# A fused attention and mixture-of-experts kernel: another order of its first loads and of its last block's tail tiles

## The chip, the cores and the metric

The kernel runs on one core of one Trainium2 chip. Its time is the device time of one execution in microseconds (us), as the median of several runs; lower is better. Five engines work side by side, each with its own queue of instructions: TensorE (PE; its weight loads are shown as PEld), VectorE (DVE), ScalarE (ACT), GpSimd (POOL) and SyncE (SP), which here issues nearly all DMA transfers. They wait for each other by semaphores. One execution was also recorded by the hardware profiler, and all rows below come from that one.

## What is computed

Three steps follow each other. Attention over 4 batches of 8 heads, 576 tokens and a head width of 64, where each query keeps only its 32 largest scores; a gated product; and a mixture of 8 experts of which each token takes one:

```python
scores = q @ k.T / sqrt(D)
kth    = partition(scores, -32)[..., -32]
attn   = softmax(where(scores >= kth, scores, -1e9))
x      = (attn @ v), heads side by side          # 2304 x 512
x      = ((x @ w_a) * (x @ w_b)) @ w_out         # inner width 1536
logits = normalized(x) @ normalized(expert_emb).T / tau
e      = argmax(logits); gate = softmax(logits)[e]
out    = gate * (relu(x @ w1[e]) @ w2[e])        # inner width 1024
```

## The kernel before

**The attention loop.** `SEQ` names eight parts, in order: block (batch) 0 to 3, with A for the first 256 queries, B for the second 256, and T for the 64 tail queries. Each part runs over four pairs of heads. One query tile of 128 scores rows against 576 keys is called an attention tile here (the code says row); there are 144, taken one per step from step −10 on. A tail tile holds both heads of a pair, 64 queries each. Each step does several things for several tiles at once: `prep` (loads of keys and queries, ten steps ahead), `split_qk` (POOL splits keys and queries into a high and a low half; for the very first part ScalarE and VectorE do it, L255, L256), `turn_qk` (TensorE transposes them, L307), `scores` (TensorE L364, ScalarE's copy L365), `topk` (VectorE's chain of four MAX8, L385, and three MATCH_REPLACE8, L388), `softmax` (ScalarE L397, POOL L400, ScalarE L402), `turn` (TensorE transposes the weights of the softmax, L419, ScalarE copies them, L422), `mix` (TensorE multiplies with v, L460, and spreads the sums, L440) and `finish` (POOL scales and splits; the halves are written to memory as `xh_d` and `xl_d`, L482 and L483). A part with tail has 320 columns in `mix`, one without has 256. `finish` of a part's fourth pair raises `ready`, the count of tokens that are complete.

**The weights.** `Blocks` loads 36 tiles of 512 KB of 64-bit weights (L512), unpacks them on VectorE, ScalarE and POOL (L532 to L539), splits them with two matmuls (L550, L551) and stores them in `wab_d`.

**The gated product.** The 2304 tokens are cut into nine groups of 256 (groups 0 to 8). `moe1` multiplies a group: for each of 12 values of f it does 24 matmuls (L683) with the weights that are loaded again from `wab_d` (L620, four buffers `wab`), and two f later six matmuls of the second product (L652, three for each of two token tiles). `background` puts these matmuls between those of the attention, as far as a budget for the step allows. A group enters its list as soon as `ready` covers it, and may begin two steps later. Its inputs are then read from `xh_d` and `xl_d` (L608), into tiles called `raw64` for odd groups and `xg` for even ones; the first matmul of a group needs the low halves. What is left after the attention runs behind it, densely.

**The router.** `route` is a generator with one stage per `yield`; `background` advances it by one stage after some amount of TensorE work. It takes a finished tile of 128 tokens: transposes (L725), logits (L730), ScalarE's copy `lg` (L733), VectorE's reciprocal, maximum and index (L735 to L740), one-hot (POOL), ranks by matmuls (L754, L755), and a scatter of token numbers into the experts' lists (POOL L770). When all 18 tiles are through, the lists are read back and the tokens of each expert are gathered (POOL L1042), while the first expert's matmuls (L1080, L1092, L1186) begin.

**What sets the order.** TensorE, VectorE, ScalarE and POOL run in the order in which the program is written. SyncE doesn't: a scheduler places the DMA issues by readiness and by a priority, which `tc.high_priority(offset=...)` raises. An issue whose tile isn't free yet holds all that stand behind it on that queue.

Of the kernel before, what the change touches and what calls it, by code (L numbers as in the profile page):

```python
# [16 lines left out]
AF = mybir.ActivationFunctionType  # L17
# [7 lines left out]
CAP = 336  # L25
GROUPS = [(256 * i, 256) for i in range(9)]
GN = 256
SEQ = "0A 0BT 1A 1BT 2A 2BT 3AT 3B"
LAG = 2
AHEAD_L = 10  # L30
TL = 4
# [43 lines left out]
FG = 100000  # L75
# [7 lines left out]
def fused_kernel(  # L83
# [18 lines left out]
    pe, dve, act, pool, sp = nc.tensor, nc.vector, nc.scalar, nc.gpsimd, nc.sync  # L102
# [43 lines left out]

    order_of_parts = [(int(x[0]), x[1:]) for x in SEQ.split()]
    blocks = {"A": range(4), "B": range(4, 8), "T": (8,)}
# [14 lines left out]
    eps = cst.tile([P, 1], F32, name="eps")  # L163
# [5 lines left out]

    enT = cst.tile([P, KC, EW], F32, name="enT")  # L170
    dve.memset(enT, 0.0)

    def en_load(mk):
        e_sb = mk.tile([P, RW], F32, name="xr")[:NE, :DM]
        sp.dma_start(e_sb, emb)
        sp.dma_start(tau1, tau.unsqueeze(0).to_broadcast([P, 1]))
        e_sq = mk.tile([P, RW], F32, name="xr")[:NE, :DM]
        e_ss = cst.tile([NE, 2], F32, name="e_ss")
        act.activation(e_sq, e_sb, AF.Square, accum_out=e_ss[:, 0:1])
        pool.tensor_tensor(e_ss[:, 1:2], e_ss[:, 0:1], half[:NE], op=OP.pow)  # L180
        return e_sb, e_ss
# [16 lines left out]
    with ExitStack() as ph:  # L198
# [72 lines left out]
        def prep(b, pr, part, n, c0):  # L271
            o = Part()
            o.b, o.pr, o.n, o.c0 = b, pr, n, c0
            o.first = now[0] + AHEAD_L
            o.lead = part == [p for bb, p in order_of_parts if bb == b][0]
            o.tail = "T" in part
            o.M = 256 if "A" in part or "B" in part else 0
            o.N = o.M + 64 * o.tail
            o.c = 2 if "B" in part else 0
            if o.lead:  # L280
                load_k(o, b, pr)
            o.qr = load_q(o)
            o.qs = None
            return o
# [426 lines left out]
        def route(ch, p):  # L711
# [20 lines left out]
            lg = mk.tile([P, NE], F32, name="lg")  # L732
            act.activation(lg, pl[:, :NE], AF.Copy)  # L733
            yield 0.0
            dve.reciprocal(st[:, 1:2], st[:, 1:2])  # L735
            m8 = mk.tile([P, 8], F32, name="m8")
            dve.max(m8, lg)
# [49 lines left out]
        made = {}  # L787
# [76 lines left out]
        for step in range(-AHEAD_L, NRW + TL + 5):  # L864
            now[0] = step
            if step + AHEAD_L < NRW:
                b, pr, part, first, last, kind, c, slot = rows[step + AHEAD_L]
                if first:
                    with tc.high_priority(offset=FG):
                        o = made[b, pr, part] = prep(b, pr, part, len(made), c0)  # L870
                        coming.append(o)
                    if pr == NP - 1:
                        c0 += o.N
# [435 lines left out]
```

## Time and profile before

| | us |
|---|---|
| median of 3 runs (1329.62 to 1331.72) | 1330.2 |
| the profiled execution | 1327.13 |
| its span, first to last instruction | 1325.2 |
| TensorE busy | 1181.8 (89%) |
| VectorE busy | 920.5 (69%) |
| ScalarE busy | 820.3 (62%) |
| POOL busy | 715.1 (54%) |

A share is a mean over the whole span; the attention takes up the first 900 us, the rest of the gated product runs to about 1040 us and the experts from there on, and each has limits of its own. The mean granted clock of TensorE was 0.956 of full speed.

### The profile page before, as it was taken

Reading aid. Unit: us, or ns where it says so; the run is one execution under the profiler, and the core shown is the slowest. Engines: PE = TensorE matmul, PEld = TensorE weight load, DVE = VectorE, ACT = ScalarE, POOL = GpSimd, SP = SyncE. Lnnn points to the kernel's source line nnn. Section 1 sums busy time; section 2 is a strip of 40 time slices with the busy share of each in tenths; the row PEclk is TensorE's granted clock in tenths of the full one; section 3 lists DMA queues with packets and bytes.
Section 4 is the critical chain, followed back from the end, with each engine's and each line's share of the span. In section 5 each row is a group of like instructions: output and inputs, shape, how many; then the busy total and the mean of one; then the engine's idle time right before and its main releaser. Section 6 shows DMA issues by size and latency. Waiting matters only on the chain. (4 is left out here: it accounts for less than half of the span.)

```text
span 1325.2 us, 23082 instructions
## 1 busy us (share of the span) xinstructions
PE 1181.8 (89%) x7828; PEld 992.9 (75%) x7829; DVE 920.5 (69%) x1991; ACT 820.3 (62%) x1953; POOL 715.1 (54%) x1160
## 2 busy tenths in 40 slices
PE   4767878987999998999999998799999989999996
PEld 3444756666888787887887787678898868888885
DVE  6989999987899988998889899750100135444440
ACT  4776888876777777776778776663532335444441
POOL 4555767755676777765767766564455321111100
PEclk9786999897999999998999999799999999999999
DMA  6333476454666666665666656457998145555520
GB/s 210 121 103 124 143 244 210 177 179 146 182 184 223 185 208 193 212 180 176 204 183 192 202 165 203 146 170 247 331 300 246 40 129 197 174 168 173 176 91 19
DMA packets 125707, 237.00 MB, mean 179 GB/s; under 512 B 22765, under 2 KB 71021, under 8 KB 125586
## 3 DMA queue, kind: packets, MB, share of 16 engines
q1 hardware_dynamic: 121426, 225.20, 53.8%
q0 software_dynamic: 4160, 10.29, 2.4%
q8 instruction: 63, 1.03, 0.3%
q14 instruction: 58, 0.48, 0.1%
HBM read 195.38 MB, written 40.85 MB: 178 GB/s over the span
## 5 line engine op out<-in xcount | busy, mean ns | idle before, releaser
L385 DVE MAX8 t<-y 128x8 f32<-128x576 f32 x432 | 312.0, 750 | 3.1
L400 POOL TENSOR_TENSOR z<-s,z 128x576 f32<-128x576 f32 x144 | 206.2, 1432 | 105.6 <-ACT z L397 103.4
L683 PE MATMUL ab<-xg,wab 128*128 128x256 f32 x1440 | 215.8, 292 | 5.6 <-ACT gab L687 3.8
L388 DVE MATCH_REPLACE8 y<-t,y 128x576 f32<-128x576 f32 x288 | 214.0, 743 | 0.0
L683 PEld LDWEIGHTS ab<-xg,wab 128*128 128x128 f32 x1440 | 190.5, 193 | 9.0 <-ACT gab L687 4.4
L683 PE MATMUL ab<-raw,wab 128*128 128x256 f32 x1152 | 173.6, 292 | 6.8 <-ACT gab L687 4.4
L419 PE MATMUL tr<-ident,z 128*128 128x128 f32 x720 | 136.0, 289 | 44.5 <-ACT z L402 36.1
L402 ACT ACTIVATE z<-z,bi 128x576 f32<-128x576 f32 x144 | 111.6, 775 | 79.5 <-POOL z L400 79.4
L683 PEld LDWEIGHTS ab<-raw,wab 128*128 128x128 f32 x1152 | 152.4, 193 | 10.8 <-ACT gab L687 5.7
L385 DVE MAX8 t<-s 128x8 f32<-128x576 f32 x144 | 107.7, 748 | 54.1 <-ACT s L365 48.8
L364 PE MATMUL tr<-kT,qT 128*128 128x288 f32 x512 | 127.8, 334 | 18.1 <-ACT s L365 13.9
L422 ACT ACTIVATE wt<-tr 128x384 f32<-128x384 f32 (+2 forms) x320 | 127.4, 413 | 17.7 <-PE tr L419 16.9
L365 ACT ACTIVATE s<-tr 128x288 f32<-128x288 f32 x288 | 118.9, 413 | 30.0 <-PE tr L364 28.6
L419 PEld LDWEIGHTS tr<-ident,z 128*128 128x128 f32 x720 | 91.6, 147 | 60.2 <-ACT z L402 39.7
L652 PE MATMUL x<-wo,gh 128*128 128x512 f32 x432 | 135.6, 395 | 0.0
L1015 DVE TENSOR_TENSOR u<-raw,u 128x1024 fp32r<-128x1024 f32 x64 | 76.2, 1221 | 83.5 <-ACT u L1014 60.6
L1064 POOL DMA_INDIRECT out_dram<-o,ids x24 | 24.0, 1000 | 200.4 <-ACT o L1063 197.1
L1092 PE MATMUL y<-u,hT 128*128 128x512 f32 (+1 forms) x528 | 128.0, 396 | 0.4 <-DVE hT L1197 0.4
L639 POOL TENSOR_TENSOR gab<-gab 128x256 f32<-128x256 f32 x108 | 81.9, 758 | 84.7 <-ACT gab L687 79.5
L364 PEld LDWEIGHTS tr<-kT,qT 128*128 128x128 f32 x512 | 89.1, 205 | 32.1 <-ACT s L365 17.5
L397 ACT ACTIVATE z<-s,bi 128x576 f32<-128x576 f32 x144 | 112.7, 783 | 0.0
L1092 PEld LDWEIGHTS y<-u,hT 128*128 128x128 f32 (+1 forms) x528 | 89.7, 173 | 27.6 <-DVE hT L1197 0.5
(178 smaller groups left out, 2211.8 us busy)
## 6 DMA issues: line engine op xcount, KB each, us to landing
wab<-wab_d SPq DMA_DIRECT2D x192, 512.0 KB
raw<-in_moe_w_dram SPq DMA_DIRECT2D x28, 1024.0 KB
wab_d<-wab SPq DMA_DIRECT2D x24, 512.0 KB
kT_d<-kT SPq DMA_DIRECT2D x16, 576.0 KB
kT<-kT_d SPq DMA_DIRECT2D x16, 576.0 KB
vs<-in_v_dram SPq DMA_DIRECT2D x32, 256.0 KB
raw<-in_moe_w_a_dram SPq DMA_DIRECT2D x12, 512.0 KB
raw<-in_moe_w_b_dram SPq DMA_DIRECT2D x12, 512.0 KB
```

The costliest lines, as they stand in the source:

```text
L364: pe.matmul(p, l, r, start=(i == 0), stop=(i == len(terms) - 1))
L365: act.activation(t.s[:, cs], p, AF.Copy, scale=SCALE)
L385: dve.max(v, cur)
L388: dve.match_replace(out=rest, in_to_replace=v, in_values=cur, imm_value=LOWEST)
L397: act.activation(t.w, t.s, AF.Relu, bias=t.bi[:, 1:2], scale=-HUGE)
L400: pool.tensor_tensor(t.w, t.s, t.w, op=OP.subtract)
L402: act.activation(t.w, t.w, AF.Exp, bias=t.bi[:, 0:1], accum_out=t.o.sm[:, t.slot : t.slot + 1])
L419: pe.transpose(pt[:, i * P : (i + 1) * P], t.w[:, k0 : k0 + P], ident)
L422: act.activation(th[:, sl, w], pv[:, :, src], AF.Copy)
L652: pe.matmul(px[t], g[:, ts], wo[:, w, f], start=(f == 0 and i == 0), stop=(f == NF - 1 and i == 2))
L683: pe.matmul(p[:, i], wt[:, a, c, :], xg[x][:, c, :], start=(j == 0), stop=(j == len(terms) - 1))
L1092: pe.matmul(p[:m], (hi, lo)[a], u[:, b, f % 4, :], start=(f == 0 and i == 0), stop=(f == NF2 - 1 and i == 2))
```

## The change

Four edits. `SEQ` ends with "3A 3BT" in place of "3AT 3B": the four tail tiles of batch 3 move from its first part to its second, so that the parts before last and last have 256 and 320 columns in place of 320 and 256. A new ScalarE instruction (an exponential of a constant, written to a place that is overwritten later) stands behind the clearing of `enT`, far ahead of ScalarE's first copy. `route` has a second `yield 0.0` behind the copy of the logits. And `prep` of the very first part runs at a four times higher priority offset.

```diff
--- before.py
+++ after.py
@@ -25,7 +25,7 @@
 CAP = 336
 GROUPS = [(256 * i, 256) for i in range(9)]
 GN = 256
-SEQ = "0A 0BT 1A 1BT 2A 2BT 3AT 3B"
+SEQ = "0A 0BT 1A 1BT 2A 2BT 3A 3BT"
 LAG = 2
 AHEAD_L = 10
 TL = 4
@@ -169,6 +169,7 @@
 
     enT = cst.tile([P, KC, EW], F32, name="enT")
     dve.memset(enT, 0.0)
+    act.activation(enT[:, 0, 0:1], eps, AF.Exp)
 
     def en_load(mk):
         e_sb = mk.tile([P, RW], F32, name="xr")[:NE, :DM]
@@ -732,6 +733,7 @@
             lg = mk.tile([P, NE], F32, name="lg")
             act.activation(lg, pl[:, :NE], AF.Copy)
             yield 0.0
+            yield 0.0
             dve.reciprocal(st[:, 1:2], st[:, 1:2])
             m8 = mk.tile([P, 8], F32, name="m8")
             dve.max(m8, lg)
@@ -866,7 +868,7 @@
             if step + AHEAD_L < NRW:
                 b, pr, part, first, last, kind, c, slot = rows[step + AHEAD_L]
                 if first:
-                    with tc.high_priority(offset=FG):
+                    with tc.high_priority(offset=FG if made else 4 * FG):
                         o = made[b, pr, part] = prep(b, pr, part, len(made), c0)
                         coming.append(o)
                     if pr == NP - 1:
```

Lines of the changed kernel are one higher from L172 on, two higher behind the router's new stage.

**SyncE at the program's start.** `raw` is a weight tile, `kr` keys, `vs` values, `qr` queries, `x1`..`x4` a count. Before:

```order
L512 DMA raw_134<-in_moe_w_a_dram 128x4x256
L241 DMA kr<-in_k_dram 128x2x256
L512 DMA raw_136<-in_moe_w_b_dram 128x4x256
L262 DMA vs<-in_v_dram 128x2x256 x2
L246 DMA kr<-in_k_dram 64x64
L266 DMA vs<-in_v_dram 64x2x64 x2
L246 DMA kr<-in_k_dram 64x64
L228 DMA qr<-in_q_dram 128x128 x4
L206 DMA ids_d<-z 128x320
L215 DMA row_d<-xr 1x516
L175 DMA xr<-in_moe_expert_emb_dram 8x512
L241 DMA kr<-in_k_dram 128x2x256
```

and now:

```order
L242 DMA kr<-in_k_dram 128x2x256
L247 DMA kr<-in_k_dram 64x64 x2
L229 DMA qr<-in_q_dram 128x128 x2
L513 DMA raw_135<-in_moe_w_a_dram 128x4x256
L513 DMA raw_137<-in_moe_w_b_dram 128x4x256
L263 DMA vs<-in_v_dram 128x2x256 x2
L242 DMA kr<-in_k_dram 128x2x256
L267 DMA vs<-in_v_dram 64x2x64
L247 DMA kr<-in_k_dram 64x64
L513 DMA raw_174<-in_moe_w_a_dram 128x4x256
L267 DMA vs<-in_v_dram 64x2x64
L247 DMA kr<-in_k_dram 64x64
```

The first part's keys with their tails and two query loads (`128x128 x2`) moved ahead of all weights. The values, the second part's keys (the second `128x2x256` of `kr`) and the third weight tile stand between them and what follows: the last key tail of the second part, the store of the first kT, and that part's queries.

**TensorE between groups 5 and 6.** L419 is a turned softmax tile (L420 now), L364 the scores (L365), L307 turned keys and queries (L308), L460 a mix, L725 and L730 the router (L726), L683 the gated product (L684). Before, behind the last L652 of group 5:

```order
L419 MATMUL tr<-ident,z 128x128 x3
L364 MATMUL tr<-kT,qT 128x288 x2
L725 MATMUL ab<-ident,xr 128x128 x4
L419 MATMUL tr<-ident,z 128x128 x2
L364 MATMUL tr<-kT,qT 128x288 x2
L307 MATMUL tr<-identr,qs 128x128 x8
L419 MATMUL tr<-ident,z 128x128 x3
L683 MATMUL ab<-xg_11093,wab 128x256 x4
L730 MATMUL ab<-enT,x1T 128x8 x4
L364 MATMUL tr<-kT,qT 128x288 x2
L419 MATMUL tr<-ident,z 128x128 x2
```

and now, behind the last of group 5:

```order
L420 MATMUL tr<-ident,z 128x128 x3
L365 MATMUL tr<-kT,qm_115 128x288 x4
L420 MATMUL tr<-ident,z 128x128 x2
L365 MATMUL tr<-kT,qm_115 128x288 x4
L308 MATMUL tr<-identr,qs 128x128 x6
L420 MATMUL tr<-ident,z 128x128 x3
L684 MATMUL ab<-xg_10790,wab 128x256 x4
L365 MATMUL tr<-kT,qT 128x288 x2
L684 MATMUL ab<-xg_10788,wab 128x256 x8
L420 MATMUL tr<-ident,z 128x128 x2
L684 MATMUL ab<-xg_10790,wab 128x256 x4
L726 MATMUL ab<-ident,xr 128x128 x4
```

The first matmuls of group 6 moved up by one attention tile, more of them follow in each tile, and the mix is no longer between them and the end of group 5.

**SyncE at the reads of the last groups' inputs.** `xh_d` and `xl_d` are the high and low halves of the attention's results. Before, when the last block's first part is done:

```order
L482 DMA xh_d_60<-xh_10937 128x320
L483 DMA xl_d_61<-xR_10957 128x320
L608 DMA xg0_11091<-xh_d_60 128x4x256
L608 DMA raw64_11099<-xh_d_60 128x4x256
L608 DMA xg1_11093<-xl_d_61 128x4x256
L608 DMA raw64_11101<-xl_d_61 128x4x256
L262 DMA vs_11287<-in_v_dram 128x2x256
L266 DMA vs_11287<-in_v_dram 64x2x64
L620 DMA wab_11317<-wab_d_62 128x1024
L620 DMA wab_11319<-wab_d_62 128x1024
```

and now, at the end of the attention:

```order
L754 DMA row_d_64<-xr_11053 128x516
L621 DMA wab_12132<-wab_d_62 128x1024
L483 DMA xh_d_60<-xh_12004 128x320
L621 DMA wab_12134<-wab_d_62 128x1024
L484 DMA xl_d_61<-xR_12024 128x320
L609 DMA raw64_12053<-xh_d_60 128x4x256
L621 DMA wab_12180<-wab_d_62 128x1024
L621 DMA wab_12182<-wab_d_62 128x1024
L609 DMA raw64_12055<-xl_d_61 128x4x256
L609 DMA xg1_12626<-xl_d_61 128x4x256
L609 DMA xg0_12624<-xh_d_60 128x4x256
```

Before, the inputs of group 6 (`xg0`, `xg1`) and of group 7 (`raw64`) are read in one row, and group 8's much later. Now group 7's (`raw64`) stand behind the very last writes of the attention, its low halves behind two weight loads, and group 8's directly behind them.

**TensorE at the end.** The ranks' matmuls (L754, L755) of the second to last tile stand behind 12 matmuls of L1080 after the last tile's logits (L730), and those of the last tile behind 12 more. Now it is 24, and 6 more.

## Rows read from the trace of the kernel before

**Rows 1.** Stretch, us, busy (count) of each engine, TensorE clock, DMA share, GB/s
```profile
20.00:100.00 80.00, 53.59 (x254) 36.15 (x254) 72.83 (x166) 57.97 (x136) 44.05 (x58) 0.79 0.42 137
...
100.00:200.00 100.00, 79.59 (x459) 58.36 (x458) 98.51 (x202) 78.89 (x182) 63.42 (x75) 0.88 0.51 168
...
700.00:800.00 100.00, 93.41 (x711) 79.22 (x712) 90.59 (x208) 74.78 (x196) 70.61 (x120) 1.00 0.62 189
...
1100.00:1200.00 100.00, 100.00 (x556) 87.51 (x555) 49.11 (x70) 45.22 (x69) 19.22 (x18) 1.00 0.52 176
```

**Rows 2.** Head: start, us, engine, line, operation, count [idle before <-releaser]
```profile
0.76 0.43 SPq L512 DMA_DIRECT2D raw<-in_moe_w_a_dram  x1
...
10.18 1.28 ACT L255 ACT_TABLE_LOAD   x1 [10.05 <-DMA kr<-in_k_dram]
...
11.48 0.68 ACT L255 ACTIVATE ks<-kr 128x576 fp32r<-128x576 f32 x1
...
13.18 0.41 SPq L241 DMA_DIRECT2D kr<-in_k_dram  x1
...
15.80 0.39 SPq L512 DMA_DIRECT2D raw<-in_moe_w_a_dram  x1
...
16.55 0.67 POOL L218 TENSOR_SCALAR ks<-kr 128x576 fp32r<-128x576 f32 x1 [3.14 <-DMA kr<-in_k_dram]
...
18.00 0.76 DVE L385 MAX8 t<-s 128x8 f32<-128x576 f32 x1 [1.34 <-ACT s L365]
...
26.25 0.40 ACT L365 ACTIVATE s<-tr 128x288 f32<-128x288 f32 x1
...
27.07 0.74 DVE L385 MAX8 t<-s 128x8 f32<-128x576 f32 x1
```

**Rows 3.** Timeline of TensorE between groups 5 and 6
```profile
824.91 0.50 PE L652 MATMUL x<-wo,gl 128*128 128x512 f32 x1 [2.96 <-POOL gl L639]
...
834.20 1.23 PE L307 MATMUL tr<-identr,qs 128*128 128x128 f32 x8 [3.90 <-ACT wt L422]
...
840.13 4.50 PE L460 MATMUL tr<-wt,vs 128*64 128x256 f32 x20
```

**Rows 4.** Busy time of two group transitions, and parts of the second
```profile
600.00:640.00 40.00, 36.03 (x251) 31.66 (x250) 31.94 (x75) 27.02 (x69) 23.01 (x42) 0.91 0.54 168
...
820.00:860.00 40.00, 28.93 (x188) 24.11 (x187) 31.74 (x76) 24.98 (x63) 21.92 (x48) 0.83 0.49 150
...
830.00:840.00 10.00, 5.70 (x29) 5.09 (x28) 8.80 (x21) 5.59 (x14) 5.38 (x13) 0.53 0.26 88
...
840.00:850.00 10.00, 9.46 (x63) 6.54 (x62) 5.03 (x12) 5.00 (x13) 4.01 (x5) 0.79 0.26 74
```

**Rows 5.** Timeline at the attention's end: TensorE and SyncE's last write
```profile
899.80 0.66 PE L440 MATMUL tr<-ident,rc 128*64 128x128 f32 x8
...
903.84 0.38 SPq L483 DMA_DIRECT2D xl_d<-xR  x1
...
905.59 3.04 PE L683 MATMUL ab<-xg,wab 128*128 128x256 f32 x24
...
908.46 0.40 PE L652 MATMUL x<-wo,gl 128*128 128x512 f32 x1
...
909.85 3.04 PE L683 MATMUL ab<-xg,wab 128*128 128x256 f32 x24
```

**Rows 6.** Timeline there: a weight load, and TensorE waiting for it
```profile
920.83 0.56 SPq L620 DMA_DIRECT2D wab<-wab_d  x1
...
926.82 1.70 PE L683 MATMUL ab<-raw,wab 128*128 128x256 f32 x12 [1.00 <-DMA wab<-wab_d]
```

**Rows 7.** Timeline of TensorE at the start of the expert phase
```profile
1047.56 1.67 PE L1080 MATMUL h<-xg,u 128*128 128x256 f32 x12
...
1073.23 5.11 PE L1186 MATMUL h<-u,xT 128*80 128x512 f32 x15 [3.85 <-DVE xT L1059]
```

**Rows 8.** Waits of VectorE; columns: us in total, times, longest us
```profile
DVE m L737 <- ACT lg L733: 40.8, 13, 11.8
```


## The prediction

> **What bounds the kernel now.** I read the busy table by stretches first [rows 1]. From 20 us to 200 us VectorE is the full engine (91%, then 98.5%), because every attention row needs its chain of top-32 searches there. Later it is TensorE: 93% busy at full clock from 700 to 800 us, and 100% in the expert phase. So a microsecond counts only where the engine that is full at that time gains or loses it: at the head that is the start of VectorE's first search, later it is a hole in TensorE's row of matmuls. The timeline of the head [rows 2] shows the first, the one of the large TensorE hole near 825 us [rows 3] and the sums of two matching stretches [rows 4] show the second. The end of the attention [rows 5, 6] and the start of the expert phase [rows 7] say what the moved work meets there. A last row [rows 8] serves the router stage.
>
> **1. The loads at the head and the table load.** Before, SyncE issues a 512 KB weight tile first (0.76 us), then the keys among more weights and values, and the queries behind them. ScalarE waits 10.05 us for the keys, and only then loads its table for 1.28 us, so its first copy starts at 11.48; the first search starts at 18.00 [rows 2]. In the changed order only the keys, their tails and two query loads (about 0.4 MB) stand ahead of the first weight tile. The keys of the second part, 256 KB, were issued at 13.18 and free POOL at 16.55, 3.4 us later, with their tails between [rows 2]. At the head of the queue they leave at about 0.8 as the first weight tile did, so I put them at 4.5 (0.8 + 3.4, rounded up). The table is loaded before that, since its new instruction needs only a constant. ScalarE's first copy then starts near 4.6 in place of 11.48: −6.9, or −7.0 with rounding, and the first search at 11.0.
>
> That gain doesn't last whole. The second part's keys have their last tail behind the third weight tile, and that one waits until the first is unpacked: before it was issued at 15.80 [rows 2]; shifted by 7 that is 8.8. A tail of v and one of keys follow (1.1 us more), and about 2.7 us of landing (less than the 3.4 above, since only the small tail is late), so 12.6 in place of 16.55: −4.0. This decides row 2 of the attention, though its keys are the first part's: its scores stand on TensorE behind the second part's key turns, and their second half behind two weight splits, whose unpacking stands on POOL behind that part's splits. Those scores were copied at 26.25 + 0.40 = 26.65, and VectorE, searching without a gap since 18.00, took them at 27.07 [rows 2]. With the first search at 11.0 it wants them at 20.1, and they come at 26.65 − 4.0 = 22.65: VectorE stands some 2.7 us, and row 2 starts near 22.9 in place of 27.07. VectorE is the full engine to 200 us at least [rows 1], and carries what is left to the end of that stretch: **−4.2**; bounds −2.5 (the small tail lands 1.7 us later still) and −7 (it lands with the rest).
>
> A rule weighs in here. The profile shows 1.28 us of table load, and the first copy at 11.48, 0.02 us after its end. The Trainium skill, page "ScalarE: Activation LUTs", section "What ACT_TABLE_LOAD costs", states about 1283 ns for the load and 1380 ns of drain on top, 2.66 us in all for a switch. The load agrees with this row, the drain doesn't appear behind it. By the page the head would gain 1.4 us more, if the second part's keys let it, and the result would be 1323.7.
>
> **2. The tail tiles of the last block.** With "3A 3BT" the part before last yields 256 tokens, not 320. Two things move.
>
> *The gap between groups 5 and 6.* Before, group 5 ends while the last block's first part is ending too. Group 6's first matmul stands two attention tiles later, and only four of its matmuls stand in the tile after that; TensorE waits 2.96, then 3.90 us, with no background work to put in; its clock falls to half (0.53 from 830 to 840), so the mix of 20 matmuls takes 4.50 us [rows 3, 4]. From 820 to 860 us TensorE has 28.93 busy us at a clock of 0.83: 40 − 28.93 × 0.83 = 16.0 us lost. In the changed order group 6 may start right where group 5 ends, because its 256 tokens are complete one part earlier. The changed program's rows there are those that this kernel already has between groups 3 and 4, 36 attention tiles earlier (the same end of one group after a mix of 320 columns, the same distance to the next one's first matmul). There, from 600 to 640 us, the loss is 40 − 36.03 × 0.91 = 7.2 us. Difference: **−8.8**. The order gives a second figure: when the last mix comes, group 6 has 40 matmuls of L683 and 9 of L652 more behind it than before. By one f of the dense stretch (24 of L683 in 908.46 − 905.59 = 2.87 us, six of L652 in 1.39 us [rows 5]) that is 40 × 0.120 + 9 × 0.232 = 6.9 us. Bounds −5 (a part of the hole opens anew) and −11.
>
> *The input of group 7.* Before, its token block was complete with the first part of the last block, and was read together with group 6's. Now the last 64 columns of the last block, which it needs, come out of the very last mix. Group 7's first matmul reads the low halves, and on SyncE's queue their read stands behind the high halves' read and behind two weight loads, whose buffers come free when group 6's last f is multiplied. After the last mix TensorE has 56 of L683 and 17 of L652 left: 56 × 0.120 + 17 × 0.232 = 10.6 us of cover. The write itself isn't late: the last one was issued 3.4 us after its part's last TensorE step ended (899.80 + 0.66 to 903.84 [rows 5]). But the second weight load waits to 10.6 − 1.4 (the six L652 at the end) = 9.2 us, and with its issue of some 0.6 the read goes out at 10.1. A 512 KB read issued at 920.83, third in a row of three, was what TensorE waited for until 926.82: 6.0 us [rows 6]. The keys above, 256 KB, needed 3.4. This read is the second of two, so I take the middle, 4.7; it is there at 14.8, and TensorE stands for 4.2 us (2.9 to 5.5). The idle stretch of 3.90 us halved the clock; the two stretches that followed lost 5.70 × 0.47 + 9.46 × 0.21 = 4.7 us to it [rows 4]. Group 7 is denser work, which is back at speed sooner, so I take a little under half, 2.1. Together **+6.3**; bounds +2.9 and, with the clock's 4.7, +10.2. Nothing can pass: TensorE's order is fixed, and behind the read stand group 8's input reads and the first expert's weights, which have 50 us of group 7 as cover.
>
> The Trainium skill, page "DMA: Bandwidth & Descriptors", section "Anatomy of one DMA", gives 2.0 us + bytes/436e3 per transfer, most of the 2.0 being the receipt of the write. By it 512 KB would land in an estimated 3.2 us, and the stand would be 2.7 us; the result would be 1323.6. The row speaks against it (6.0 us in that company), so the row decides.
>
> **3. One more router stage.** The vector work on a tile's logits comes one step after ScalarE's copy. VectorE waited for these logits 40.8 us in 13 places, the longest 11.8 [rows 8], but some of these lie behind the attention, where VectorE has time, and the others lie where TensorE is the full engine, since the first router tile comes only with the end of group 0's second product. TensorE hardly waits for a threshold there. I take **0**, bounds −2 (some of the waits do reach TensorE) and +1 (a router tile ends later).
>
> At the end it costs. The one-hot matmul of the second to last router tile slides behind 12 more of L1080, which take 1.67 us [rows 7]. Its scatter, the last one's (the scatters follow each other), the read of the lists and the gather slide with it. TensorE already waits 3.85 us at 1073.23 for what comes out of this chain, and is full from there on. So that wait grows by about **+1.6** (0 if the lists' own wait takes it up, to +2.5).
>
> **The sum.** −4.2 − 8.8 + 6.3 + 1.6 = −5.1. The profiled execution took 1327.1 (a span of 1325.2), 3.1 under the median of the runs; from it 1322.0 would follow, from the median **1325.1**.
>
> **The rivals.** (a) *Group 7's input is in time.* If the read of the low halves lands before the last L652 ends, the 6.3 goes: −11.4, 1318.8. For it: the write is out 7 us before it is needed; against it: two weight loads stand in front. (b) *No measurable change.* The read lands at its slowest, 6.0, and the clock falls as at 834 us: 5.5 + 4.7 = 10.2 in place of 6.3, so −1.2, 1329.0. It decides from a wait and clock loss of 8.7 us together. (c) *Slower, by a crowded queue.* The low halves come as the third of three 512 KB reads in a row. At the 150 GB/s that the stretch 820 to 860 moved [rows 4], 1.57 MB take 10.5 us; TensorE stands 10.1 + 10.5 − 10.6 = 10.0, plus 4.7 of clock: 14.7, and the sum is +3.3, 1333.5. It decides from a landing of about 10 us on; the row above showed 6.0. (d) *The change doesn't do what it says*: the keys come no earlier, since all transfers share the same 16 engines. Then only the table's 1.28 us is left at the head in place of 4.2: −2.2, 1328.0. The changed queue speaks against it, as only 0.4 MB stand ahead.
>
> **How the numbers follow.** A measurement of this kernel can tell about 0.2%, 2.7 us, from no change. Chances: the forecast 0.48, (a) 0.17, (b) 0.15, (c) 0.13, (d) 0.07. The forecast and (a) are faster by over 0.2%: 0.65. (b) and (d) are within it: 0.22. (c) is slower: 0.13. The range goes from 1316.0, which is (a) with the head's gain at its larger bound (−7 in place of −4.2), to 1331.5, which takes in (b) with the head at its smaller bound and the tail at its larger one; (c) stays out.
>
> **What would show it.** Right: ScalarE's first copy under 5.5 us and the first search at 10 to 12; the third row's first search at 22 to 23.5; no TensorE wait over 3 us between groups 5 and 6; a wait of 3 to 6 us at group 7's first L684, released by a read of the low halves, with the clock down behind it; at the first expert's second matmul row a wait of 5 to 6 us. Wrong: group 7 starts without a wait (a); its wait is 8 us or more (c); row 2's search starts later than 25 (the head's gain is gone); or the head's gain is lost again while VectorE is full, which would make term 1 nothing.

## The result: slower, and the profile after

The changed kernel takes 1338.7 us (median of 6) against 1329.9 (median of 6 of the kernel before, on the same chip): a ratio of 1.0058, 95% interval 1.0032 to 1.0083. It is 8.8 us slower; 1325.1 was forecast, with 1316.0 to 1331.5 as range. The profiled execution took 1337.0 (span 1335.2) against 1327.1 before.

The head did mostly what was forecast. ScalarE and VectorE in the timeline of the changed kernel (start, us, engine, line, operation, [idle before <- releaser]), which answer to [rows 2]:

```profile
0.76 1.28 ACT L172 ACT_TABLE_LOAD   x1 [0.63 <-PEq L1291]
...
4.04 0.68 ACT L256 ACTIVATE ks<-kr 128x576 fp32r<-128x576 f32 x1 [1.78 <-DMA kr<-in_k_dram]
...
10.87 0.76 DVE L386 MAX8 t<-s 128x8 f32<-128x576 f32 x1 [1.04 <-ACT s L366]
...
24.42 0.76 DVE L386 MAX8 t<-s 128x8 f32<-128x576 f32 x1 [4.41 <-ACT s L366]
```

The table is loaded while the keys travel, the first search starts at 10.87 in place of 18.00, and that of the third tile (row 2) at 24.42 in place of 27.07: of 7.1 us at the first tile 2.65 are left at the third. The rest is lost in the 4.41 us for which VectorE waits for that tile's scores.

The hole between groups 5 and 6 [rows 3, 4] is half closed. Busy time of the changed kernel (stretch, its length, busy us of PE, PEld, DVE, ACT, POOL, then granted clock, DMA share, GB/s):

```profile
820.00:860.00 40.00, 35.09 (x247) 28.46 (x248) 28.68 (x67) 26.62 (x66) 22.62 (x46) 0.91 0.40 122
```

TensorE loses 40 − 35.09 × 0.91 = 8.1 us here in place of 16.0, and no wait there is over 2.40. But group 7's first matmul then waits longer than any matmul did between 300 and 1110 us before (3.90). TensorE, POOL and SyncE of the changed kernel:

```profile
902.48 0.92 PE L441 MATMUL tr<-ident,rc 128*64 128x128 f32 x12
...
905.96 0.88 POOL L473 TENSOR_TENSOR xsb<-xsb,xR 128x320 f32<-128x320 f32 x1
906.79 0.19 POOL L753 TENSOR_TENSOR xr<-st,eps 128x1 f32<-128x1 f32 x1
...
907.80 0.46 POOL L219 TENSOR_SCALAR xh<-xsb 128x320 fp32r<-128x320 f32 x1
...
908.54 0.88 POOL L221 TENSOR_TENSOR xR<-xsb,xh 128x320 fp32r<-128x320 f32 x1
...
909.45 0.32 SPq L484 DMA_DIRECT2D xl_d<-xR  x1
912.65 0.57 SPq L609 DMA_DIRECT2D raw<-xh_d  x1
913.31 1.04 SPq L621 DMA_DIRECT2D wab<-wab_d  x2
915.81 0.55 SPq L609 DMA_DIRECT2D raw<-xl_d  x1
...
922.79 5.08 PE L684 MATMUL ab<-raw,wab 128*128 128x256 f32 x24 [8.43 <-issue]
```

The last mix ends on TensorE at 903.40 (L441). Its output is split by POOL. SyncE issues the last write at 909.45 and the reads at 912.65 (high halves) and 915.81 (low halves), and TensorE stands 8.43 us, to 922.79. What SyncE waited for between 900 and 925 us (us in total, times, longest):

```profile
SPq L609 <- DMA xh_d<-xh: 2.9, 1, 2.9
SPq L609 <- DMA xl_d<-xR: 1.4, 1, 1.4
```

So each read goes out when the write of its block has landed: that of the high halves took 4.3 us from issue to landing, that of the low halves 6.3. The two weight loads between the reads were issued by 914.35, before the second write had landed. For TensorE's wait the profile says "issue": it shows no releaser. That it is the read issued at 915.81 is inferred from its being the last input to be read. The clock is at half when the work begins again:

```profile
917.00:927.00 10.00, 4.21 (x20) 0.50 1.07 368
900.00:1040.00 140.00, 126.83 (x862) 0.94 0.84 263
```

(here with PE as the only engine). From 927 to 932 us it is 0.97 again; the mean of 0.94 also holds a later fall, to 0.83 between 960 and 980. The kernel before had 132.11 busy us at a clock of 1.00 from 900 to 1040.

These two agree with the reading that the late input paid the hole back. They don't show where the rest of the 14 us between forecast and result lies; the experiments show most of it.

### The profile page after: what moved, and what is told of

Its sections match the earlier page's. It is cut to its first block, busy times and chain, and to the rows that moved or that the text cites. A ratio compares the mean times of both kernels' runs of the same rounds, so it can differ in the third digit from the quotient of the medians.

```text
span 1335.2 us, 23073 instructions
## 1 busy us (share of the span) xinstructions
PE 1187.5 (89%) x7828; PEld 997.1 (75%) x7829; DVE 919.3 (69%) x1991; ACT 820.5 (61%) x1954; POOL 716.8 (54%) x1160
## 5 line engine op out<-in xcount | busy, mean ns | idle before, releaser
L684 PE MATMUL ab<-xg,wab 128*128 128x256 f32 x1440 | 214.2, 291 | 3.3 <-ACT gab L688 3.3
L684 PEld LDWEIGHTS ab<-xg,wab 128*128 128x128 f32 x1440 | 189.6, 193 | 6.5 <-ACT gab L688 4.3
L684 PE MATMUL ab<-raw,wab 128*128 128x256 f32 x1152 | 174.5, 294 | 16.3 <-issue 8.4
L420 PE MATMUL tr<-ident,z 128*128 128x128 f32 x720 | 135.9, 289 | 38.6 <-ACT z L403 33.6
L684 PEld LDWEIGHTS ab<-raw,wab 128*128 128x128 f32 x1152 | 154.4, 196 | 21.2 <-ACT gab L688 9.5
L365 PE MATMUL tr<-kT,qT 128*128 128x288 f32 x512 | 127.6, 333 | 20.8 <-ACT s L366 13.6
L653 PE MATMUL x<-wo,gh 128*128 128x512 f32 x432 | 138.2, 402 | 0.0
L420 PEld LDWEIGHTS tr<-ident,z 128*128 128x128 f32 x720 | 92.3, 147 | 53.1 <-ACT z L403 36.7
L365 PEld LDWEIGHTS tr<-kT,qT 128*128 128x128 f32 x512 | 88.5, 204 | 35.1 <-ACT s L366 17.0
```

The lines of the kernel that those rows point to most:

```text
L365: pe.matmul(p, l, r, start=(i == 0), stop=(i == len(terms) - 1))
L420: pe.transpose(pt[:, i * P : (i + 1) * P], t.w[:, k0 : k0 + P], ident)
L653: pe.matmul(px[t], g[:, ts], wo[:, w, f], start=(f == 0 and i == 0), stop=(f == NF - 1 and i == 2))
L684: pe.matmul(p[:, i], wt[:, a, c, :], xg[x][:, c, :], start=(j == 0), stop=(j == len(terms) - 1))
```

## The experiments

Each ratio is to the kernel before on the same chip, with a 95% interval; a rounded difference in us behind it (+5) is this ratio's, and others are between medians. The letters in the expectations: A says that the SEQ edit (the last block's tail tiles) is the whole loss, B that the router stage is; C that the head's gain stays.

### The three edits one at a time

seq_only:
```
-SEQ = "0A 0BT 1A 1BT 2A 2BT 3AT 3B"
+SEQ = "0A 0BT 1A 1BT 2A 2BT 3A 3BT"
```


> Only the order of the last block's parts is changed (tail tiles in its second part); loads at the head, table and router stage are as before. Theory A (the tail tiles' move is the whole loss): in the changed kernel TensorE stood 8.4 us at group 7's first matmul and ran 2.0 us slower behind it, and the attention ended only about 4 us better off in work done; so this alone is +7 to +11 us against the kernel before, with a wait of 7 us or more at group 7's first matmul. Rival B (the router stage is the loss, because it shifts work all along the attention): this alone is within 3 us of before.

Measured: 1333.2 us, 1.0037 [1.0017, 1.0057], +5.

head_only (the table's instruction and the first part's loads):
```
+    act.activation(enT[:, 0, 0:1], eps, AF.Exp)
-                    with tc.high_priority(offset=FG):
+                    with tc.high_priority(offset=FG if made else 4 * FG):
```


> Only the two head edits (first part's loads ahead of all, table loaded early). Theory A: row 2's first search is 2.6 us earlier as in the changed kernel, and of that about 0 to 2 us is left at the end: -2 to 0 us. Rival C (what VectorE gains at the head stays): -2.6 to -4 us. Rival D (the earlier start costs later, by weights that aren't ready): +1 us or more.

Measured: 1325.1 us, 0.9977 [0.9960, 0.9994], −3, as C expected.

route_only:
```
             act.activation(lg, pl[:, :NE], AF.Copy)
             yield 0.0
+            yield 0.0
```


> Only the added router stage. Theory A: 0 to +2.5 us, all of it at the start of the expert phase (the wait before the first expert's second row of matmuls 3.85 us before, 5 to 6 us here). Rival B: +5 us or more, lost in the attention.

Measured: 1339.5 us, 1.0092 [1.0068, 1.0115], +12.

no_seq (head and router stage, the old SEQ):


> Everything but the move of the tail tiles (head edits and router stage together). Theory A: the sum of those two runs, -2 to +2 us against before, and no wait over 2 us where group 7 begins. Rival B: +4 us or more.

Measured: 1338.8 us, 1.0074 [1.0045, 1.0104]. Theory A falls: without the SEQ edit the kernel is as slow as with it. The router stage, which the prediction had put at 0 in the attention, is the largest single loss. B doesn't hold alone either, since the SEQ edit costs 5 us. The single effects, −3 + 5 + 12, sum to 14, with about ±5 from their intervals, and the whole change costs 8.8 ± 3: a difference that isn't clear of noise. By the profiled executions they nearly add. POOL's product of the last attention tile (L400) comes 2.8 us earlier in head_only, 2.7 earlier in seq_only and 7.4 later in route_only, which makes +1.9, and in the changed kernel it came at 891.85 in place of 891.19, +0.7. What follows it took 0.3 us less, 7.6 more and 2.9 more, which makes +10.2, and in the changed kernel +9.3.

### Which of the shifted instructions costs

An added stage shifts everything behind it: VectorE's search of the logits, the one-hot and its matmul, the rank's copy, POOL's work and the scatter of ids. Theory S says that the scatter's new place beside the attention's POOL work is the cost, V that VectorE's is, N that the number of stages at the end is.

stage_scat (the stage just ahead of the scatter instead):
```
             act.activation(rk[:, NE:], rk[:, :NE], AF.Copy, accum_out=st[:, 5:6])
             yield 0.0
+            yield 0.0
```


> The router's extra stage stands ahead of the scatter (POOL's transfer of token numbers into the lists) in place of behind the logits' copy; all other router work stays where it was, only the scatters come one stage later. In the run with the added stage alone (+12 us) the attention lost its time in steps of 1.1 to 2.2 us at tiles 57, 77, 104, 113, 122 and 130, which are the tiles at which the scatters stand there. Theory S (the scatter's place among the softmax steps on POOL's fixed order costs): nearly the same loss, +7 to +12 us, with steps at the same tiles. Rival V (VectorE's maximum and index in their new place cost): within 3 us of before. Rival N (the number of stages at the end costs): +2 to +4 us, none of it in the attention.

noscat (the first 11 scatters left out) and noscat_stage (the same with the stage of the change):
```
-            pool.indirect_dma_start(
+            if ch > 10:
+                pool.indirect_dma_start(
```


> The first 11 scatters, those inside the attention, are left out (so these tokens' results are missing), no stage is added. Theory S: two of these stand straight ahead of a softmax step in the kernel before, at about 1.6 us each: -2 to -6 us. Rival V and N: within 1.5 us of before.

> The same 11 scatters left out, and the router's extra stage behind the logits' copy in. Theory S: the added stage now costs little in the attention, so 0 to +4 us against the kernel without scatters and without the stage, most of it at the start of the expert phase. Rival V: the full +12 us of the stage against that kernel stay. Rival N: +2 to +4 us, like S; the other two runs tell these two apart.

Measured: stage_scat 1332.1, 1.0022 [1.0003, 1.0041]; noscat 1322.9, 0.9947 [0.9927, 0.9967]; noscat_stage 1331.5, 1.0025 [1.0008, 1.0042]. The 11 scatters cost 6 to 7 us, the most that S had expected, but without them the stage still costs 8.6 us (between the last two), where S had expected 0 to 4. S falls. The 3 us of stage_scat are what N expected.

stage_post (the stage behind VectorE's work):
```
             dve.tensor_scalar(st[:, 2:3], m8[:, 0:1], st[:, 1:2], -1.0, op0=OP.mult, op1=OP.mult)
             yield 0.0
+            yield 0.0
```


> The extra router stage behind VectorE's work on the logits and not ahead of it, so VectorE's five instructions keep their old place, while everything behind them (exp, one-hot, rank matmuls, scatter) comes a stage later, as in the change. Rival V (VectorE's new place is what costs) expects a time within 0.25% of the kernel before, with at most the tail's 2.8 us. Theories P and L (the later places of the rank matmuls and of what follows) expect +8 to +13 us, ratio 1.006 to 1.010, as with the stage alone.

stage_notail (the stage, but not for the last two router tiles):
```
+            if ch < 2 * len(GROUPS) - 2:
+                yield 0.0
```


> The extra router stage alone, but not for the last two router tiles, whose chain ends the router's work after the attention. If the tail takes 2.8 us of the stage's 12 (what the trace of the stage alone shows between the last attention tile and the expert phase), this one is 8 to 10 us above the kernel before, ratio 1.006 to 1.0075; if the tail is nothing, 1.008 to 1.0105; if the stage's cost lies in the tail after all, within 0.2%.

Measured: stage_post 1337.3, 1.0056 [1.0037, 1.0076]; stage_notail 1338.2, 1.0065 [1.0046, 1.0083]. V falls: VectorE's instructions at their old place don't save the kernel. N falls as well: with the last two router tiles left as they were, 9 of the stage's 12 us stay, and in the trace the last attention tile's product on POOL comes at 900.68 in place of 891.19. So these 9 are lost in the attention. The other 3 are within the noise of the two ratios, which come from two chips. One sees how far the cause was from VectorE's wait in [rows 8]: that wait did shrink between 300 and 905 us, and the kernel became slower. In the kernel before, then with the stage alone:

```profile
DVE m L737 <- ACT lg L733: 24.4, 8, 8.9
```

```profile
DVE m L738 <- ACT lg L733: 4.5, 3, 3.3
```

### Two buffers, shared

The waits of TensorE between 300 and 905 us (us in total, times, longest), in the kernel before:

```profile
PE tr L364 <- ACT s L365: 11.8, 11, 1.6
PE ab L683 <- ACT gab L687: 8.1, 7, 3.1
...
PE x L652 <- POOL gl L639: 4.3, 3, 3.0
```

and with the stage alone:

```profile
PE ab L683 <- ACT gab L687: 13.0, 8, 3.1
PE tr L364 <- ACT s L365: 12.6, 11, 2.0
PE x L652 <- POOL gl L639: 6.3, 5, 3.0
```

L683 is the gated product of a group, L687 ScalarE's copy of it. Its wait grows most, by 4.9 us. The same place in the timeline of TensorE and ScalarE, in the kernel before:

```profile
802.16 0.78 ACT L402 ACTIVATE z<-z,bi 128x576 f32<-128x576 f32 x1 [3.38 <-POOL z L400]
802.21 1.68 PE L683 MATMUL ab<-raw,wab 128*128 128x256 f32 x12
```

and with the stage alone:

```profile
807.71 0.78 ACT L402 ACTIVATE z<-z,bi 128x576 f32<-128x576 f32 x1 [2.93 <-POOL z L400]
...
808.86 0.59 ACT L687 ACTIVATE gab<-ab 128x512 f32<-128x512 f32 x1
809.34 0.18 ACT L758 ACTIVATE rk<-ab 128x16 f32<-128x16 f32 x1
...
809.50 1.81 PE L683 MATMUL ab<-raw,wab 128*128 128x256 f32 x12 [2.19 <-ACT gab L687]
```

A router tile's three TensorE results (transposes, logits, ranks) are drawn from the same set of two buffers, "ab", as the gated product. Where one of them, here the ranks (L758 copies them out), falls between two products, it takes the second buffer, and the next product cannot start before ScalarE has copied the last one. That copy stands in ScalarE's queue behind an exp which waits 2.93 us for POOL. Before, the exp waited for POOL as well (3.38 us), but no rank stood there, and L683 started without a wait. With two buffers for products alone TensorE would be a whole product ahead. Theory P says that this is the cost; rival L that the stages' places in the queues cost, whatever the buffers.

tr_ctl (the control: while the attention runs, the router's results go into the attention's four-buffer set; TensorE's order is unchanged) and tr_stage (the same with the stage):
```
-            pt = mp.tile([P, 512], F32, name="ab", bufs=2)
+            pt = ps.tile([P, 512], F32, name="tr", bufs=NTR)    # pl, pr likewise
```


> The kernel before, with the router's three TensorE results (transposes, logits, ranks) written, while the attention runs, into the four-buffer set that the attention's transposes and scores use, and no longer into the two buffers of the gated product; the order of TensorE's instructions is the same. It is the control of tr_stage. Theory P (the extra router stage costs time since the router's results share the gated product's two buffers, so that a new f waits for ScalarE to copy the last product out) expects 'PE ab <- ACT gab' to fall from 8.1 us to about 4 between 300 and 905 us, and a time of -4 to +2 us against the kernel before (ratio 0.997 to 1.0015), since the four-buffer set loses a little. Rival L (the buffers don't matter, only where the stages stand in TensorE's row) expects no change beyond 0.2%.

> The same with the extra router stage, its only difference from tr_ctl. The stage alone cost 12 us (ratio 1.0092) on the shared buffers. Theory P expects most of it gone: +2 to +5 us against tr_ctl (2.8 us of it in the tail, where the edit is as before), a difference of the two ratios of 0.0015 to 0.004, and PE's waits 'ab <- ACT gab' no more than 2 us above the control's. Rival L expects the whole cost again: +8 to +13 us against tr_ctl, a difference of 0.006 to 0.010.

after_tr (the whole change with those buffers):


> The whole change, with the router's three TensorE results in the attention's four-buffer set while the attention runs (as in tr_ctl and tr_stage). Theory P (the stage's cost in the attention comes from sharing the gated product's two buffers): after stood 8.8 us above the kernel before, and in tr_stage the stage's 12 us had shrunk to -1.2 (tr_stage less tr_ctl); so after less 8 us and plus the control's 3 to 4: ratio 1.000 to 1.004. Rival L (the later places cost, as tr_stage's one profiled execution shows: 5.6 us late at the last attention tile, its control 0.2): no gain, ratio 1.005 to 1.009.

Measured: tr_ctl 1332.4, 1.0030 [1.0012, 1.0049]; tr_stage 1331.1, 1.0014 [0.9998, 1.0031]; after_tr 1330.7, 1.0016 [0.9997, 1.0035]. On separate buffers the stage costs nothing (−1.2 us to its control, +12 on shared ones), and the whole change falls from 1.0058 to 1.0016, although the four-buffer set itself costs 3 to 4 us. Rival L had expected +8 to +13 us to the control and 1.005 or more for after_tr, and misses both. P misses two of its three numbers as well: tr_ctl is slower than its 1.0015, and the stage costs less than its +2 to +5; after_tr is within its range. The wait between 300 and 905 us is small too, tr_stage:

```profile
PE ab L683 <- ACT gab L687: 2.0, 1, 2.0
```

Three things keep this from being a proof. First, tr_ctl has none of this wait left and is still 3 to 4 us slower than before: TensorE waits for the four-buffer set instead, tr_ctl:

```profile
PE tr L364 <- ACT wt L422: 7.3, 4, 3.8
PE tr L419 <- ACT s L365: 5.3, 3, 2.1
```

(the kernel before has no such rows). Second, in the changed kernel itself the wait on the two buffers is 9.8 us, only 1.7 above before, and a larger one, L653 for POOL's `gl`, went from 4.3 to 9.4 and is as large in after_tr; so there the buffers' share rests on the times alone. Third, in the one profiled execution of tr_stage, POOL's product of the last attention tile comes at 896.79, of tr_ctl at 891.36 (before: 891.19, stage alone: 898.55). By these traces the stage would still be 5.4 us late there. The profiled execution of tr_ctl was the fastest of its 12, so I go by the medians; but what share is left to the places alone isn't settled by this pair.

### The same stage at other places

The number RGAP says after how much background work on TensorE (2 us) the next router stage is issued. gap_17 and stage_gap17:
```
-RGAP = 2
+RGAP = 1.7
```


> No extra stage; the distance between two router stages, counted in TensorE's background work, is 1.7 us in place of 2, so that all stages stand at other places and each router tile ends a little sooner. Rival L (any shift of the stages from their old places costs, since these were found by search) expects +4 to +12 us, ratio 1.003 to 1.009. The theory that the longer chain of stages is what costs expects no loss or a small gain, ratio 0.997 to 1.0015.

> The extra router stage together with the shorter distance of 1.7 us, so that a router tile's whole chain is about as long as before (ten stages of 1.7 for nine of 2). The theory that the chain's length costs expects most of the stage's 12 us back: ratio 0.998 to 1.003. Rival L and theory P (places, buffers) expect a number with no relation to the length; if gap_17 is near the kernel before, they expect this one still at 1.005 or more.

Measured: gap_17 1333.4, 1.0015 [0.9995, 1.0035]; stage_gap17 1324.4, 0.9962 [0.9943, 0.9980]. Without the stage the shorter distance gains nothing; with it the kernel is some 16 us faster than with the stage at the old distance (each against before on its own chip), and faster than before. Both expectations for stage_gap17 were missed. TensorE's wait in stage_gap17, between 300 and 905 us:

```profile
PE ab L683 <- ACT gab L687: 2.6, 4, 0.8
```

So the extra stage isn't bad in itself: its price goes from +12 us to −7 by the distance alone, on shared buffers. What costs is where the ten stages of a tile then fall in the queues. The buffer wait isn't the whole of it: in gap_17 it is as small (2.8 us), and that kernel isn't faster than before. A shorter chain explains gap_17 no better. Since the places alone can move the stage's price this far, and the separate buffers also move them, that the stage costs nothing there may in part be another such shift; no run excludes it.

### Group 7's input

seq_data (the SEQ edit, with group 7 reading group 6's tokens, which are complete):
```
-                        sp.dma_start(t[:, :, :N].bitcast(F32), d[:, :, g0 : g0 + N])
+                        sp.dma_start(t[:, :, :N].bitcast(F32), d[:, :, g0 - N * (self.gi == 7) : g0 + N * (self.gi != 7)])
```


> The SEQ edit alone, with group 7 reading group 6's tokens, so that its read needn't wait for the last block's last columns; the instructions and their number are those of seq_only, and the later tokens' results are not the reference's. Theory A (the hole between groups 5 and 6 is won, and group 7's late input gives it back) expects group 7's first L684 to wait less than 1 us and the clock to hold: seq_only's +5 less 6 us of standing and 2 us of clock, so -1 to -6 us against the kernel before, ratio 0.9955 to 0.9992. The rival (the SEQ edit loses inside the attention, by the longer second part) expects still +2 us or more, ratio over 1.0015.

Measured: 1328.5 us, 0.9992 [0.9975, 1.0009]; group 7's first matmul starts without a wait. Against seq_only that is 6 us: the late input is what made the SEQ edit slower than before (6.07 us of standing in seq_only), and without it the edit stands at about −1, at the weak end of A's range. So the gain of the hole, some 8 us in its own stretch, hardly shows at the end. In its one profiled execution it is lost again behind the attention: TensorE's waits from 903 to 1110 us, first of the kernel before, then of seq_data:

```profile
PE ab L683 <- DMA wab<-wab_d: 4.0, 5, 1.1
```

```profile
PE ab L683 <- DMA wab<-wab_d: 7.2, 6, 2.7
...
PE tr L1055 <- DMA xg<-row_d,ids: 2.2, 2, 1.4
```

The groups behind the attention wait longer for their weights, and the experts now wait for the gather (L1055), which had been in time before. TensorE's clock from 1040 to 1100 us is 0.91 in place of 0.97.

### Versions that beat both

head_two (the head's edits, but with the loads of the first two parts ahead of the weights):
```
+                    with tc.high_priority(offset=FG if len(made) > 1 else 4 * FG):
```


> The head edits, but with the loads of the first two parts ahead of all else, in place of the first part's alone; no other edit. With the first part's alone VectorE stood 4.4 us at the third attention tile, because the second part's keys came late. Theory A (the second part's keys bound row 2): that wait goes to under 1.5 us and the third tile's first search starts near 21 in place of 24.4; -4 to -7 us against before. Rival C (what is gained there is lost to weights that come later): no better than the run with the first part alone, -1 to -3.5 us.

best_gap17 (head_two, the router stage, RGAP = 1.7) and all_gap17 (the same with the SEQ edit, that is the whole change with two numbers altered):


> head_two's head (the table called early, the loads of the first two parts ahead of the weights), the extra router stage, and the stages' distance of 1.7 us; the last block's tail tiles stay in its first part. If the two gains lie at different places of the program and add up, -6.5 and -5 give -11.5 us against the kernel before, ratio 0.989 to 0.993. If the earlier head only shifts into later waits, as it partly did in the changed kernel, ratio 0.994 to 0.997.

> The whole change with the loads of the first two parts ahead of the weights and the stages' distance of 1.7 us. Against best_gap17 it differs by the SEQ edit alone, which cost 5 us alone. If group 7's late input stands apart from the router's places, it costs 3 to 7 us here too: ratio 0.993 to 0.998. If its loss came by the router's places, it costs nothing here (within 2 us of best_gap17).

Measured: head_two 1322.3, 0.9951 [0.9935, 0.9967]; best_gap17 1320.6, 0.9931 [0.9911, 0.9951]; all_gap17 1315.0, 0.9896 [0.9874, 0.9917]. VectorE in head_two:

```profile
14.05 0.74 DVE L386 MAX8 t<-s 128x8 f32<-128x576 f32 x1
...
23.10 0.74 DVE L386 MAX8 t<-s 128x8 f32<-128x576 f32 x1
```

The first search starts later than in the changed kernel (14.05, not 10.87), and the third tile's earlier (23.10, not 24.42; near 21 was expected), with no wait ahead of it; the gain is twice as large.

all_gap17 beats best_gap17 by 5.6 us (0.0035 in the ratios, give or take 0.003), and the SEQ edit is their only difference. I had expected +3 to +7 or nothing. The same edit that costs 5 us alone gains about as much here. Group 7's input now comes nearly in time (1.19 us of standing in place of 6.07 in seq_only), which by its size can be most of the difference; no run separates it. TensorE, POOL and SyncE of all_gap17:

```profile
887.07 0.92 PE L441 MATMUL tr<-ident,rc 128*64 128x128 f32 x12
...
889.03 0.87 POOL L473 TENSOR_TENSOR xsb<-xsb,xR 128x320 f32<-128x320 f32 x1
889.99 0.46 POOL L219 TENSOR_SCALAR xh<-xsb 128x320 fp32r<-128x320 f32 x1
890.53 0.88 POOL L221 TENSOR_TENSOR xR<-xsb,xh 128x320 fp32r<-128x320 f32 x1
...
891.72 0.38 SPq L484 DMA_DIRECT2D xl_d<-xR  x1
892.21 0.37 SPq L621 DMA_DIRECT2D wab<-wab_d  x1
893.87 0.57 SPq L609 DMA_DIRECT2D raw<-xh_d  x1
894.73 0.55 SPq L609 DMA_DIRECT2D raw<-xl_d  x1
...
899.77 1.67 PE L684 MATMUL ab<-raw,wab 128*128 128x256 f32 x12 [1.19 <-DMA raw<-xl_d]
```

Here no router step stands among the three POOL steps of the last split, no weight load stands between the two reads, and the two writes land in 3.4 and 2.9 us. From the end of the last mix to the low halves' read it is 894.73 − 887.99 = 6.7 us; in the changed kernel it was 915.81 − 903.40 = 12.4. TensorE stands 1.19 us, and the profile names the read of the low halves as what ended it. The clock holds:

```profile
820.00:900.00 80.00, 78.16 (x567) 0.97 0.59 182
900.00:1040.00 140.00, 132.43 (x937) 1.00 0.73 242
```

## Why the prediction was wrong, step by step

**The head (term −4.2): right in its mechanism, a little large.** head_only measured −3.1; in the changed kernel row 2's search came at 24.42 (22.9 forecast, 22 to 23.5 as the test). The first search was forecast to 0.1 us (11.0, 10.87). The step from there failed in its size: POOL's split of the second part's keys was to start 4.0 us earlier, at 12.6, and started at 14.34, which is 2.2 earlier. The logic that this part decides row 2 was right: head_two, which puts that part's loads ahead too, doubles the gain.

**The hole between groups 5 and 6 (−8.8): right in its stretch, wrong as a price of the whole.** The loss from 820 to 860 us fell from 16.0 to 8.1, that is −7.9. But seq_data, in which group 7's input isn't late, measured −1 for the SEQ edit (interval −3.3 to +1.2). The step counted the time won in one stretch as won at the end, and left out that what comes behind then waits more: for weights (7.2 us in place of 4.0) and for the experts' gather (2.2 in place of none).

**Group 7's input (+6.3): the right wait, half its size.** TensorE stood 8.43 us where 4.2 was forecast, outside the bounds 2.9 to 5.5. Two figures of the step failed, and the way of one. "The read goes out at 10.1" (its own terms, 9.2 and 0.6, make 9.8): it went out 12.4 us after the last mix. The text took the write's issue from before (3.4 us after the mix [rows 5]); it was at 909.45, 6.0 after, since the split's first POOL step began 2.6 us after the mix and four router steps and one of the gated product stand between that step and the end of the split. It said that the write "isn't late" by its issue and put its landing at nothing. What held the read was not the weight loads but this landing: 6.3 us, to 915.8. "So I take the middle, 4.7" for the landing: 922.79 − 915.81 = 7.0, more than the 6.0 of [rows 6]. The clock's share came out: the first product took 929.10 − 922.79 = 6.31 us where a dense one takes 4.26 [rows 5], 2.05 more (2.1 forecast, a choice that no row before had shown). By the sign "its wait is 8 us or more" this was rival (c), which had 0.13; but (c) drew it from a landing of about 10 us, and the landing was 7.0. Alone the step was nearer: in seq_only the read went out 10.9 us after the last mix and TensorE stood 6.07 us, and against seq_data the late input is worth 6 us (give or take 3).

**The router stage (0 in the attention, bounds −2 to +1; +1.6 in the tail): this step failed, and it is the largest part of the miss.** The text argued from VectorE's wait alone, "TensorE hardly waits for a threshold there", and took the stage as a shift of VectorE's five instructions. Every later step of a router tile shifted with them, on TensorE, ScalarE, POOL and SyncE's queue, and the ranks among them hold one of the two buffers of the gated product. Alone the stage costs +12 us, of which 9 lie in the attention, where 0 had been put. For the tail's 1.6 the runs are too noisy. TensorE's wait for a first expert's input grew, from 3.85 [rows 7] to 4.77, and two waits for the gather came ahead of it:

```profile
1074.58 0.47 PE L1057 MATMUL tr<-ident,xg 80*128 80x80 f32 x4 [1.26 <-DMA xg<-row_d,ids]
1075.92 0.66 PE L1057 MATMUL tr<-ident,xg 128*128 128x128 f32 x4 [0.88 <-DMA xg<-row_d,ids]
...
1082.29 1.14 PE L1188 MATMUL h<-u,xT 128*80 128x512 f32 x2 [4.77 <-DVE xT L1061]
```

The one wait is under the 5 to 6 us that were to show it; the three together grew by 3.1. The stage isn't shown as their cause: in seq_only, without it, the same waits are 5.0 and 1.6 us.

**The sum.** Of the forecast's terms the head was −4.2 and measured −3, the SEQ edit −2.5 (−8.8 + 6.3) and measured +5, the stage +1.6 and measured +12. Adding prices of separate edits was no large error here, but it isn't safe: the SEQ edit measures +5 alone, between the two on top of head and stage (1.0058 against 1.0074, not clear of noise), and −5.6 on top of the shorter stage distance. The router's steps stand among those that decide how late group 7's input is (four of them in the last split), and they had been counted as free. No rival named the router stage as a loss, so none of the four held its mechanism.

**What stays open.** How the stage's 9 us in the attention divide between the shared buffers and the other queues. That the buffers have a share is what two pairs of times suggest, tr_stage and after_tr; that other places matter too is shown by gap_17 and stage_gap17. No run here separates them place by place, and a profiled execution lay up to 5 us from its kernel's median, as much as these effects.

## What to carry to other kernels

Where background steps are dealt out between other work by a counter, one more step moves all later ones, on every engine: list for each what buffer it holds and which queue it stands in before calling it free, and try the counter's setting together with the edit. The whole change lost 8.8 us with the old setting and gained 14.7 with another one and one more part's loads at the head. When a block goes through memory to the next stage, count the whole path: the engine steps that stand among its splits, the issue of the write, its landing, and the read. And time won in a hole counts only as far as the work behind it is ready to start sooner.

## What the runs showed of the hardware

The trip through memory was longer than I had assumed, and a read went out only when its write had landed: from the issue of a write to the issue of the read of the same block 893.87 − 890.48 = 3.4 us (all_gap17, high halves), 912.65 − 908.29 = 4.4 us (changed kernel, high halves) and 915.81 − 909.45 = 6.4 us (low halves). The high halves' writes:

```profile
890.48 1.15 SPq L483 DMA_DIRECT2D xh_d<-xh  x1
```

```profile
908.29 0.32 SPq L483 DMA_DIRECT2D xh_d<-xh  x1
```

After a stand of 8.43 us TensorE's granted clock was 0.50 from 917 to 927 us, that is 1.2 GHz, the lower of its two levels, then 0.97 to 932, and the first 24 matmuls took 5.08 us where the dense ones of [rows 5] took 3.04.
